# A mixture-of-experts kernel: small tables moved between partitions by ScalarE copies instead of products with selecting matrices

## The chip, the cores and the metric

The kernel runs on one core of one Trainium2 chip. The metric is the device time of one execution in microseconds (us); lower is better. Times of a kernel are given as the median of several runs, and one further execution is profiled.

## What is computed

A linear attention (eight batches, eight heads, 576 positions, 64 wide) is normalised by its root mean square and read as 4608 rows x of 512 numbers. A gating layer then decides for each row whether it is worked on at all, and which one of eight experts works on it:

```
kv  = einsum('bhsd,bhse->bhde', k, v)
o   = einsum('bhsd,bhde->bhse', q, kv)
x   = (o / sqrt(mean(o*o) + 1e-6) * g_norm)         # as rows: 4608 x 512
out = x
for rows with x @ w_skip > 0:
    e    = argmax(x @ w_gate);  gate = softmax(x @ w_gate)[e]
    out += gate * (relu(x @ w1[e]) @ w2[e])          # 512 -> 1024 -> 512, eight experts
```

## The kernel before, in words

**Attention, 0 to about 119 us.** Batches are streamed in; TensorE makes the states and the values, ScalarE squares and copies, VectorE normalises, GpSimd applies `g_norm`. The rows x are stored to `out` by SyncE's queue (lines 640 and 651) and in part by GpSimd's. The gating decisions are ranked on the way, so that at the end every chosen row has a slot of its expert.

**The experts, about 119 to 371 us.** They are done in the order of their number of rows, position r = 0 to 7. An expert's slots are cut into pieces of 128 rows, and at the end pieces of 64 or 32 rows (`PIECES`, line 279). For each piece GpSimd gathers rows of x from `out` by an indirect DMA (line 1153), TensorE transposes them (`expert_in`, line 1157), ScalarE copies the transposed tile to SBUF (lines 879 and 881), TensorE makes layer 1 and layer 2, VectorE multiplies by the gate and adds x (`result`, line 1389), and GpSimd scatters the rows back (line 1392). Expert 0 runs plainly (`layer_1`, line 1181, with a relu on ScalarE at line 1183; `layer_2`, line 1193). Experts 1 to 7 use sums of blocks, Strassen-like (`fast_1`, `fast_2`, products at line 1261), for which VectorE makes sums of weights (`w1_sums`, line 1203, `w2_sums` and `x_sums`, line 1209) and adds partial products in PSUM (line 1265); ScalarE holds copies of partial products (line 1271).

**Two tables by slot.** `srow` (128 partitions x 24 columns; column r * 3 + c is slots 128c to 128c+127 of expert r) holds the row number of each slot; `gate` holds its gate. Both come from products that place values in slots (`place`, line 760), summed by VectorE (line 818). For a piece of 128 rows that begins at a multiple of 128, its column is the list of rows as it stands. There are nine pieces for which it isn't: one of 128 rows that begins 64 slots into a column, and eight of 64 or 32 rows. A piece of 64 rows is spread over 128 partitions as two halves of each row, one of 32 rows as four quarters, so the same 64 or 32 numbers have to stand in two or four places down the partitions. `again_of(table, which)` (lines 1104 to 1124) makes these nine columns. Pieces with the same place and size make one run, of which there are five, in dictionary order: (64, 128) with one column, (64, 32) with two, (0, 64) with one, (0, 64) with two, (0, 32) with three.

In the kernel before, `again_of` writes the columns into PSUM by TensorE: for each of the four runs of 64 or 32 rows one fp32 product with a matrix `again` of 0 and 1 that selects and repeats partitions, and for the run of 128 rows two products with shifted parts of the identity. Each fp32 product shows as two rows in the profile, so one full call is 12 rows for the products and 12 for their weight loads (line 1120).

**Who calls it, and in what order.** The order of work on each engine is written by hand (`tc.manual_schedule`): every engine takes its instructions in the order in which the Python code issues them. Near the end of the attention (lines 1541 to 1563) the order is: layer 1 of expert 0 for hidden blocks 4 and 5 on the first 192 slots; `place` and `layer_2` parts; `add_pieces` completes `srow`; then `again_rows(..., range(0, 2))` for the runs that expert 0 needs soon, `slot_rows`, block 6 of layer 1, `again_rows(..., range(2, 5))`, block 7 of layer 1, nine gathers on GpSimd, more of layer 2, `gates()` (an Exp on ScalarE with a table load before it, and a chain on VectorE), and the transposes of expert 0's last two pieces. `again_rows` turns a moved column into row numbers for the cut rows, `arows` (line 1136) and `asrc` (line 1138), on VectorE.

In `experts`, for r = 0: `first_tables` runs layer 1 of expert 0 for the remaining slots with the two gate placements between; the result of piece 0; `expert_in` for expert 1's first two pieces; then `again_gates` (line 1576), which calls `again_of` for all runs and copies the nine columns from PSUM to SBUF as `agate`; the result of piece 1, which needs `agate`; on VectorE the eight `w1_sums` of expert 1; `expert_in` for expert 1's other two pieces; layer 2 of expert 0; and on VectorE the four `x_sums` of expert 1, before the results of expert 0's last two pieces.

Of the kernel before, what the change touches and what calls it, by code (L numbers as in the profile page):

```python
# [8 lines left out]
FP32 = mybir.dt.float32  # L9
# [8 lines left out]
def kernel(  # L18
# [43 lines left out]
    nc = tc.nc  # L62
# [3 lines left out]
    P = 128  # L66
# [28 lines left out]
    gat_pool = ctx.enter_context(tc.tile_pool(name="gat", bufs=1))  # L95
# [14 lines left out]
    g_ps = ps_g.tile([P, 512], FP32)  # L110
    GB = 4 * KD + 8 * G
# [89 lines left out]
    ident = keep.tile([P, P], FP32)  # L201
# [31 lines left out]
    for a in range(2):  # L233
        r = slice(a * 64, (a + 1) * 64)
        nc.vector.tensor_scalar(out=gw_b[r, :, a, :, :],
                                in0=wraw[r, :, :].rearrange("e n (u w) -> e u w n", u=2),
                                scalar1=gcol[r, 0:1], scalar2=None, op0=ALU.mult)
# [27 lines left out]
    for i, qs in enumerate((slice(0, 4 * NQ), slice(4 * NQ, FQ))):  # L265
        nc.vector.tensor_scalar(out=row_i[:, :, qs, :], in0=row_i[:, :, qs, :],
                                scalar1=upper[:, i:i + 1], scalar2=None, op0=ALU.subtract)
# [21 lines left out]
    runs = {}  # L289
    for r, off, m in sorted(res, key=lambda x: (x[0] > 0, x[1] < KEPT, x[0])):  # L290
        col = r * CK + off // P
        at_0 = r == 0 and off < 2 * P
        runs.setdefault((off % P, m, at_0), []).append((col, r, off))
    again, part_of = {}, {}
    for lo, m, _ in runs:

        if m < P and (lo, m) not in again:
            t = keep.tile([P, P], FP32, name=f"again{lo}_{m}")
            again[lo, m] = t
            for i in range(P // m):  # L300
                nc.vector.tensor_copy(out=t[:, i * m:(i + 1) * m], in_=ident[:, lo:lo + m])
        if m not in part_of:
            q_i = setup.tile([P, 1], I32, name=f"q_i{m}")
            nc.vector.tensor_single_scalar(out=q_i[:, :], in_=part_i[:, :],
                                           scalar=m.bit_length() - 1, op=ALU.arith_shift_right)
            q_f = keep.tile([P, 1], FP32, name=f"q_f{m}")
            nc.vector.tensor_single_scalar(out=q_f[:, :], in_=q_i[:, :], scalar=float(N * P // m),
                                           op=ALU.add)
            part_of[m] = q_f
    NRES = len(res)  # L310
# [7 lines left out]
    srow = keep.tile([P, NCOL], FP32)  # L318
# [3 lines left out]
        out=srow[:, :].rearrange("p (r c) -> p r c", c=CK),  # L322
        in0=beyond[:, :].unsqueeze(1).to_broadcast([P, E, CK]),
# [496 lines left out]
    def slot_rows(cols, pool, tag):  # L820

        n = cols.stop - cols.start
        rows = pool.tile([P, n], I32, tag=f"rows{tag}", name="rows")
        nc.vector.tensor_single_scalar(out=rows[:, :], in_=srow[:, cols], scalar=float(N),
                                       op=ALU.add)
        src = pool.tile([P, n], I32, tag=f"src{tag}", name="src")
        nc.vector.scalar_tensor_tensor(out=src[:, :], in0=rows[:, :], scalar=N, in1=rows[:, :],
                                       op0=ALU.is_lt, op1=ALU.mult)
        return rows, src
# [115 lines left out]
    for b in range(KNOWN // S // 4 * 4, KNOWN // S):  # L945
        nc.gpsimd.dma_start(
            out=out[b * S:(b + 1) * S, :].rearrange("(p c) d -> p c d", c=C)[:, C - 1, :],
            in_=zero)
# [18 lines left out]
    for b, n in starts.items():  # L967
        if b:
            step, counts = portions[b]
            i = 0  # L970
# [89 lines left out]
    with tc.tile_pool(name="wpool_b", bufs=1, reuse_waits="tile") as wpool_b, \  # L1060
# [40 lines left out]

        SOON = 2

        def again_of(table, which):

            ps = g_ps[:, GB:GB + NRES]
            i = 0
            for j, ((lo, m, _), cols) in enumerate(runs.items()):
                if j not in which:
                    i += len(cols)  # L1110
                    continue
                n = len(cols)
                col = cols[0][0]
                step = cols[1][0] - col if n > 1 else 1
                if m < P:
                    parts = [(slice(0, P), again[lo, m][:, :], col)]
                else:
                    parts = [(slice(0, P - lo), ident[:, lo:P], col), (slice(P - lo, P), ident[:, 0:lo], col + 1)]
                for to, lhsT, c in parts:
                    nc.tensor.matmul(out=ps[to, i:i + n], lhsT=lhsT,  # L1120
                                     rhs=table[:, c:c + (n - 1) * step + 1:step],
                                     start=True, stop=True, skip_group_check=True)
                i += n
            return ps

        def again_rows(rows, src, which):

            ps = again_of(srow, which)
            i = 0
            for j, ((_, m, _), cols) in enumerate(runs.items()):  # L1130
                n = P // m
                cs = slice(i, i + len(cols))
                i += len(cols)
                if j not in which:
                    continue
                nc.vector.tensor_scalar(out=rows[:, cs], in0=ps[:, cs], scalar1=float(n),
                                        scalar2=part_of[m][:, 0:1], op0=ALU.mult, op1=ALU.add)
                nc.vector.scalar_tensor_tensor(out=src[:, cs], in0=rows[:, cs], scalar=N * n,
                                               in1=rows[:, cs], op0=ALU.is_lt, op1=ALU.mult)
# [296 lines left out]
        def experts(pieces, widths, srcs, xt, ht, yps0, tables, group):  # L1436

            for r in range(E):
# [17 lines left out]
                if r == 0:  # L1456
                    if yps0 is not None:
                        tables = first_tables(lambda fs: layer_1(r, xt, ht, slice(KEPT, end), fs),
                                              tables)
                        result(first[0], yps0[0], xgs[0], tables, group)  # L1460
                    else:
                        layer_1(r, xt, ht, slice(0, end), range(FC))
                    enter(more[0:2])
                    if yps0 is not None:
                        tables = again_gates(tables)
                        result(first[1], yps0[1], xgs[0], tables, group)
                    do(w1_sums(r + 1))
                    enter(more[2:])
                else:
                    fast_1(r, xt, ht, end // 2, w2_sums(r), lambda: enter(more[0:1]))  # L1470
                    enter(more[1:])
# [77 lines left out]
        arows = gat_pool.tile([P, NRES], I32, tag="arows", name="arows")  # L1549
        asrc = gat_pool.tile([P, NRES], I32, tag="asrc", name="asrc")  # L1550
        again_rows(arows, asrc, range(0, SOON))
        rows, src = slot_rows(slice(0, NCOL), gat_pool, "")
        first_1(range(6, 7))
        again_rows(arows, asrc, range(SOON, len(runs)))
        first_1(range(7, FC))
        for r in range(3):
# [18 lines left out]

        def again_gates(tables):
            agate = slot_pool.tile([P, NRES], FP32, tag="agate", name="agate")
            nc.vector.tensor_copy(out=agate[:, :], in_=again_of(tables[0][1], range(len(runs))))
            return tables[0], (tables[1][0], agate)
        experts(plan, CAPS, (src, asrc), xt0, ht0, yps0, (rows, arows), "first")  # L1580

# [5 lines left out]
        with tc.If(n_rounds > 1):  # L1587
            with tc.For_i(1, n_rounds, 1):
# [8 lines left out]
                    out=left[:, :].rearrange("p (r c) -> p r c", c=CK),  # L1597
                    in0=number_f[:, :].unsqueeze(1).to_broadcast([P, E, CK]),
                    in1=caps[:, :].unsqueeze(2).to_broadcast([P, E, CK]), op=ALU.is_ge)
                nc.vector.tensor_tensor(out=srow[:, :], in0=srow[:, :], in1=left[:, :], op=ALU.mult)  # L1600
                rows, src = slot_rows(slice(0, NCOL), slot_pool, "")
# [35 lines left out]
```

## Time and profile before

| | before |
|---|---|
| median of 4 runs | 374.5 us (373.69 to 377.35) |
| the profiled execution, its own time | 373.73 us |
| its span, first to last instruction | 371.9 us |
| TensorE clock granted | 0.998 |
| busy: PE / VectorE / ScalarE / GpSimd | 360.6 / 242.8 / 145.5 / 118.8 us |
| products at line 1120 for `srow` | 12 rows, 127.9 to 130.2 us |
| products at line 1120 for `gate` | 12 rows, 149.8 to 150.8 us |
| copies that build the `again` matrices, line 301 | 10 on VectorE, 10.5 to 11.8 us |
| `agate` copy, line 1578 | 1 on VectorE, 169 ns, at 151.1 us |

How to read it: times in the trace are microseconds from the start of the span. PE is TensorE's products and PEld its weight loads, which overlap the products; DVE is VectorE, ACT ScalarE, POOL GpSimd, SP SyncE; a q behind an engine's name is its sequencer or DMA queue. A row of a timeline gives start, duration, engine, line, operation, what is written and read, and in brackets how long the engine was idle before and what ended the wait. The ends of PE's products are modelled, and some records can be missing.

### The profile page before, as it was taken

Reading aid. Unit: us, or ns where it says so; the run is one execution under the profiler, and the core shown is the slowest. Engines: PE = TensorE matmul, PEld = TensorE weight load, DVE = VectorE, ACT = ScalarE, POOL = GpSimd, SP = SyncE. Lnnn points to the kernel's source line nnn. Section 1 sums busy time; section 2 is a strip of 40 time slices with the busy share of each in tenths; the row PEclk is TensorE's granted clock in tenths of the full one; section 3 lists DMA queues with packets and bytes.
Section 4 is the critical chain, followed back from the end, with each engine's and each line's share of the span. In section 5 each row is a group of like instructions: output and inputs, shape, how many; then the busy total and the mean of one; then the engine's idle time right before and its main releaser. Section 6 shows DMA issues by size and latency. Waiting matters only on the chain.

```text
span 371.9 us, 9717 instructions
## 1 busy us (share of the span) xinstructions
PE 360.6 (97%) x3859; PEld 314.9 (85%) x3859; DVE 242.8 (65%) x630; ACT 145.5 (39%) x398; POOL 118.8 (32%) x189
## 2 busy tenths in 40 slices
PE   8999999899999998999999999999999999999994
PEld 4788998798879768589879987998988998999983
DVE  3355557767878661866847585776876876868831
ACT  2467677666767032123303511431430440441420
POOL 7036467655777071223022303303202202102003
PEclk9999999999999999999999999999999999999999
DMA  8999999999687459954617264563672672700001
GB/s 269 386 385 389 390 384 397 395 382 332 192 305 285 113 150 361 379 186 153 226 44 261 64 228 143 195 248 82 235 249 64 234 244 78 244 3 36 22 1 54
DMA packets 32808, 81.71 MB, mean 220 GB/s; under 512 B 3242, under 2 KB 3250, under 8 KB 32756
## 3 DMA queue, kind: packets, MB, share of 16 engines
q1 hardware_dynamic: 28944, 69.48, 52.8%
q0 software_dynamic: 3792, 11.53, 9.3%
q8 instruction: 32, 0.52, 0.5%
q14 instruction: 20, 0.16, 0.1%
q10 hardware_dynamic: 20, 0.02, 0.0%
HBM read 66.80 MB, written 14.48 MB: 219 GB/s over the span
## 4 chain that ended last, share of the span: by engine, by line
PE 83%; issue 6%; DMA 5%; DVE 2%; ACT 2%; POOL 1%; SPq 1%; POOLq 0%; DVEq 0%; ACTq 0%
PE bank L1261 45%; PE bank L1193 9%; PE o_ps L499 7%; PE sum_ps L380 4%; PE bank L1181 4%; PE q_ps L461 3%; PE bank L1162 2%; DMA v<-in_v_dram 2%; PE g_ps L394 2%; DMA q<-in_q_dram 2%; DMA k<-in_k_dram 1%; PE o_ps L480 1%; PE g_ps L857 1%; PE g_ps L412 1%; PE q_ps L857 1%
## 5 line engine op out<-in xcount | busy, mean ns | idle before, releaser
L1271 ACT COPY p<-bank 128x128 f32<-128x128 f32 (+6 forms) x70 | 20.8, 297 | 99.1 <-PE bank L1261 97.3
L1261 PE MATMUL bank<-xt,w 128*128 128x128 f32 (+5 forms) x336 | 55.5, 288 | 0.6 <-DVE bank L1265 0.6
L1392 POOL DMA_INDIRECT out_dram<-xg,rows x14 | 14.0, 999 | 115.4 <-DVE xg L1389 113.1
L616 POOL TENSOR_TENSOR xb<-xl,g_b 128x512 f32<-128x512 f32 x34 | 41.3, 1214 | 29.6 <-DVE rs L537 27.7
L1261 PEld LDWEIGHTS bank<-xt,w 128*128 128x128 f32 x336 | 47.0, 190 | 2.5 <-DVE bank L1265 1.8
L1265 DVE TENSOR_TENSOR bank<-bank,p 128x128 f32<-128x128 f32 (+6 forms) x70 | 23.6, 337 | 30.2 <-PE bank L1261 28.9
L499 PE MATMUL o_ps<-kvd,qT 128*128 128x146 f32 x240 | 36.0, 290 | 0.9 <-issue 0.7
L1261 PE MATMUL bank<-xs,s 128*128 128x128 f32 (+5 forms) x224 | 36.7, 288 | 0.0
L523 DVE TENSOR_REDUCE rs<-sq 128x8 f32<-128x512 f32 x36 | 24.5, 682 | 14.8 <-ACT sq L515 14.8
L499 PEld LDWEIGHTS o_ps<-kvd,qT 128*128 128x128 f32 x240 | 31.6, 189 | 1.6 <-issue 0.9
L1261 PEld LDWEIGHTS bank<-xs,s 128*128 128x128 f32 x224 | 31.1, 190 | 1.0 <-issue 0.5
L1193 PE MATMUL bank<-w,ht 128*32 128x128 f32 (+2 forms) x424 | 29.9, 313 | 0.0
L546 DVE TENSOR_TENSOR xl<-o_ps,rs 128x584 f32<-128x584 f32 x32 | 24.5, 767 | 4.3 <-DVE rs L537 0.5
L1193 PEld LDWEIGHTS bank<-w,ht 128*32 128x32 f32 (+2 forms) x424 | 18.2, 119 | 10.7 <-issue 7.6
L1261 PE MATMUL bank<-t,ht 128*128 128x256 f32 x112 | 27.0, 384 | 0.0
L1261 PE MATMUL bank<-w,ht 128*128 128x256 f32 x112 | 26.5, 380 | 0.0
L1153 POOL DMA_INDIRECT xg<-out_dram,src x14 | 14.2, 1017 | 37.3 <-DMA out_dram<-xg,rows 13.0
L515 ACT ACTIVATE sq<-o_ps 128x512 f32<-128x512 f32 x34 | 20.3, 596 | 15.0 <-PE o_ps L499 14.9
L380 PE MATMUL sum_ps<-v,k 64*64 64x64 f32 x1152 | 25.3, 222 | 0.5 <-DMA v<-in_v_dram 0.5
L1261 PE MATMUL bank<-t,hs 128*128 128x256 f32 x112 | 25.3, 379 | 0.0
L380 PEld LDWEIGHTS sum_ps<-v,k 64*64 64x64 f32 x1152 | 21.6, 134 | 3.9 <-issue 1.4
L1261 PEld LDWEIGHTS bank<-t,ht 128*128 128x128 f32 x112 | 20.8, 190 | 3.9 <-issue 1.2
(224 smaller groups left out, 677.4 us busy)
## 6 DMA issues: line engine op xcount, KB each, us to landing
w<-in_moe_w_dram SPq DMA_DIRECT2D x16, 2048.0 KB
k<-in_k_dram SPq DMA_DIRECT2D x32, 288.0 KB
v<-in_v_dram SPq DMA_DIRECT2D x32, 288.0 KB
q<-in_q_dram SPq DMA_DIRECT2D x32, 288.0 KB
out_dram<-xb SPq DMA_DIRECT2D x29, 256.0 KB
out_dram<-xb POOLq DMA_DIRECT2D x7, 256.0 KB
xg<-out_dram,src POOLq DMA_INDIRECT x16, 3.7
out_dram<-xg,rows POOLq DMA_INDIRECT x16, 2.4
```

Of the source, the lines that this page charges most:

```text
L380: nc.tensor.matmul(out=sum_ps[w * 64:(w + 1) * 64, a, u, :], lhsT=kt[r, 2 * u + w, c, :], rhs=vt[r, 2 * u + w, c, :], start=(c == 0), stop ...
L499: mm = nc.tensor.matmul(out=ps[:, w, 0:2 * PK].rearrange("p (r k) -> p r k", r=2)[:, :, cols], lhsT=qT[:, w, a, :], rhs=kvds[b % KVD][:, u ...
L515: nc.scalar.activation(out=sq[:, :, :, :], in_=heads(ps, G, G + 2 * D), func=ACT.Square)
L523: nc.vector.tensor_reduce(out=rs[:, :, :], in_=sq[:, :, :, :].rearrange("p x y (a d) -> p x (y a) d", a=2), axis=AX.X, op=ALU.add)
L546: nc.vector.tensor_tensor(out=xl[:, :, :, :].rearrange("p x y (a k) -> p x (y a) k", a=2), in0=ps[:, :, 0:2 * PK].rearrange("p x (h k) -> ...
L616: late.append((lambda eng: eng.tensor_tensor(out=xb[:, :, 4 * u * D:(4 * u + 4) * D].rearrange("p r (w x) -> p r w x", w=2), in0=xl[:, :, ...
L1153: nc.gpsimd.indirect_dma_start(out=x_of(xg, off, m), out_offset=None, in_=cut_rows(m)[:, :], in_offset=bass.IndirectOffsetOnAxis(ap=idx[:, ...
L1181: nc.tensor.matmul(out=hps[:, cols], lhsT=w_sb[r][0][:, dc, f * P:(f + 1) * P], rhs=xt[:, dc, cols], start=(dc == 0), stop=(dc == DC - 1))
L1193: nc.tensor.matmul(out=yps[q * m:(q + 1) * m, 0:n], lhsT=ht(f)[:, off:off + m], rhs=w_sb[r][1][:, f, q * n:(q + 1) * n], start=(f == 0), s ...
L1261: nc.tensor.matmul(out=out, lhsT=lhsT(i), rhs=rhs(i), start=start and i == 0, stop=i == k - 1, skip_group_check=True)
L1265: nc.vector.tensor_tensor(out=to, in0=x, in1=y, op=ALU.add)
L1271: nc.scalar.copy(out=t, in_=x)
```

## The change

`again_of` no longer uses TensorE. It takes a tile in SBUF and fills it with ScalarE copies from one group of partitions to another: two copies for the run of 128 rows (its two halves), two for each run of 64 rows, four for each run of 32. That is 14 small copies in a full call, each of 32 or 64 partitions by one to three columns. `again_rows` gets a new tile `moved` and reads it where it read PSUM; `again_gates` has the copies write `agate` itself, so VectorE's copy from PSUM goes. Of the `again` matrices only (0, 64) is still made, since `early` (line 932) uses it; the matrices for (64, 32) and (0, 32), four VectorE copies each, are gone.

```diff
-        if m < P and (lo, m) not in again:
+        if (lo, m) == (0, 64) and (lo, m) not in again:
             t = keep.tile([P, P], FP32, name=f"again{lo}_{m}")
...
-        def again_of(table, which):
-
-            ps = g_ps[:, GB:GB + NRES]
+        def again_of(to, table, which):
+
             i = 0
             for j, ((lo, m, _), cols) in enumerate(runs.items()):
-                if j not in which:
-                    i += len(cols)
-                    continue
                 n = len(cols)
-                col = cols[0][0]
-                step = cols[1][0] - col if n > 1 else 1
-                if m < P:
-                    parts = [(slice(0, P), again[lo, m][:, :], col)]
-                else:
-                    parts = [(slice(0, P - lo), ident[:, lo:P], col), (slice(P - lo, P), ident[:, 0:lo], col + 1)]
-                for to, lhsT, c in parts:
-                    nc.tensor.matmul(out=ps[to, i:i + n], lhsT=lhsT,
-                                     rhs=table[:, c:c + (n - 1) * step + 1:step],
-                                     start=True, stop=True, skip_group_check=True)
+                if j in which:
+                    col = cols[0][0]
+                    step = cols[1][0] - col if n > 1 else 1
+                    if m < P:
+                        parts = [(q * m, lo, m, col) for q in range(P // m)]
+                    else:
+                        parts = [(0, lo, P - lo, col), (P - lo, 0, lo, col + 1)]
+                    for at_p, from_p, rows, c in parts:
+                        nc.scalar.copy(out=to[at_p:at_p + rows, i:i + n],
+                                       in_=table[from_p:from_p + rows, c:c + (n - 1) * step + 1:step])
                 i += n
-            return ps
...
-            ps = again_of(srow, which)
+            moved = gat_pool.tile([P, NRES], FP32, tag=f"moved{which.start}", name="moved")
+            again_of(moved, srow, which)
...
-                nc.vector.tensor_scalar(out=rows[:, cs], in0=ps[:, cs], scalar1=float(n),
+                nc.vector.tensor_scalar(out=rows[:, cs], in0=moved[:, cs], scalar1=float(n),
...
             agate = slot_pool.tile([P, NRES], FP32, tag="agate", name="agate")
-            nc.vector.tensor_copy(out=agate[:, :], in_=again_of(tables[0][1], range(len(runs))))
+            again_of(agate, tables[0][1], range(len(runs)))
```

## The prediction, made before the result was known

> **What bounds the kernel now.** I read the page's head first, then the chain of work that ended last, then the timeline around the three places that the diff touches. The head says which engine cannot give anything away:
>
> ```profile
> span 371.9 us, 9717 instructions
> PE 360.6 (97%) x3859; PEld 314.9 (85%) x3859; DVE 242.8 (65%) x630; ACT 145.5 (39%) x398; POOL 118.8 (32%) x189
> ...
> PE 83%; issue 6%; DMA 5%; DVE 2%; ACT 2%; POOL 1%; SPq 1%; POOLq 0%; DVEq 0%; ACTq 0%
> ```
>
> TensorE is busy 97% of the span and is 83% of the chain that ended last. A product taken off it is worth its full time unless something else is then late; ScalarE, at 39%, is where the work goes. The chain, asked for 126 to 152 us, shows the removed products on it, at line 1120:
>
> ```profile
> 128.08 0.38 PE g_ps L1120 x5
> 128.46 1.41 PE bank L1181 x8
> 129.87 0.56 PE g_ps L1120 x6
> 130.43 1.41 PE bank L1181 x8
> 131.84 3.43 PE bank L1193 x8
> 135.27 0.55 PE bank L1162 x5
> 135.82 1.88 PE bank L1193 x16
> 137.69 3.47 PE bank L1181 x26
> 141.16 0.56 issue
> ...
> 149.85 1.20 PE g_ps L1120 x12
> ```
>
> The reader is to see two things. The products cost 0.38 + 0.56 + 1.20 = 2.14 us of the chain. And from 141 to 143 us TensorE stands still for reasons the profile calls "issue": 0.56, 0.18 and 0.42 us, 1.16 in all, while the table by stretches gives the DMA engines a busy share of 0.94. The timeline then shows what lies beside the products (VectorE, GpSimd, and ScalarE's wait):
>
> ```profile
> 129.91 0.33 ACT L1183 ACTIVATE ht<-bank 128x192 f32<-128x192 f32 x1 [7.11 <-PE bank L1181]
> 131.71 0.94 POOL L1153 DMA_INDIRECT xg<-out_dram,asrc  x1 [0.30 <-issue]
> 149.45 1.07 ACT L879 COPY xt<-bank 128x512 f32<-128x512 f32 x2 [0.76 <-PE bank L1162]
> 151.28 0.48 DVE L1389 SCALAR_TENSOR_TENSOR xg<-bank,agate,xg 128x256 f32<-128x256 f32 x1
> 159.54 0.75 DVE L1389 SCALAR_TENSOR_TENSOR xg<-bank,agate,xg 128x512 f32<-128x512 f32 x1 [1.13 <-PE bank L1193]
> 161.99 0.35 DVE L1265 TENSOR_TENSOR bank<-bank,p 128x172 f32<-128x172 f32 x1 [1.05 <-PE bank L1261]
> ```
>
> ScalarE is idle for 7.11 us before 129.91, and from 151.9 to 161.3. VectorE, between the `agate` result at 151.28 and the first partial sum of expert 1 at 161.99, is idle for 1.13, 0.29 (before the result at 160.58) and 1.05 us: 2.47 us of slack.
>
> **The price of one copy.** No row of before copies a few columns of SBUF to other partitions. The nearest are these, from the timeline of ScalarE:
>
> ```profile
> 6.62 0.16 ACT L224 COPY gcol<-o_ps 128x1 f32<-128x1 f32 x1 [2.91 <-PE o_ps L220]
> 6.82 0.30 ACT L226 COPY w<-gcol 128x128 f32<-128x128 f32 x1
> 7.53 0.27 ACT L229 COPY g_b<-o_ps 128x128 f32<-128x128 f32 x1 [0.42 <-PE o_ps L227]
> 60.31 0.38 ACT L406 COPY kvd<-g_ps 64x36 f32<-64x36 f32 x2
> ```
>
> One column from PSUM takes 0.16 us; 128 columns take 0.30 from SBUF and 0.27 from PSUM, so SBUF as the source adds 0.03: 0.19 us. The pair at line 406 writes two different partition halves and takes 0.38 together, so those two do not overlap; the next copy after line 224 starts 0.20 after it, 0.04 behind its end. I take 0.19 + 0.025 = 0.215 us from one copy to the next. The low end is 0.18 (four relus at line 1183 in 0.85 us, 0.29 each, so 0.18 from start to start); the high end is 0.37, the 64x256 copies of line 387, far larger than these.
>
> Here a rule weighs against the change. The Trainium skill, "VectorE: DVE Perf Modes", section "Two Vector instructions with no wait between them", says of VectorE that an instruction whose operands start in another group of 32 partitions than the one before starts only when all before it have finished; it is stated for VectorE alone, but the pair at line 406 behaves like it. "ScalarE: Activation LUTs", section "What ACT_TABLE_LOAD costs", gives 186 ns plus 0.833 ns an element with an overlap of about 93 ns back to back: by that, without the rule, 14 copies would be an estimated 1.4 us; with the rows above they are 3.0.
>
> **The change part by part.** *Set-up.* Eight copies of about 0.17 us leave VectorE at 10.5 to 11.8 us. The chain there is input DMAs until 20.9 us: nothing. If that cover were gone it would be a gain of 0.7.
>
> *Rows, first call (6 copies).* TensorE gives back 0.38. The copies wait for `srow` (126.6) on an idle ScalarE and take 6 x 0.215 = 1.3, to 127.9; VectorE's wait for TensorE ended at 128.50, so `asrc` comes about as early or 0.5 earlier. Queued behind them on ScalarE is the relu at 129.91, which they miss by 2 us. The gathers gain nothing: `asrc` was complete at 129.24, over a microsecond before the first gather started (130.36), and the gather reads `out`, whose last stores SyncE issued at 125.3 to 126.6.
>
> *Rows, second call (8 copies).* TensorE gives back 0.56. The copies stand between the relus of blocks 6 and 7: from about 129.85 they run 8 x 0.215 = 1.7, to 131.6. The relu of block 7 (131.88 before) could come at 130.9 and comes at 131.6; its reader, the last of the four pairs of 0.43 each at line 1193, needs it at about 132.9. Exp and its table load follow at 131.9, not later than the 132.2 of before. The `asrc` columns from this call are first read by the fifth gather, at 135.5, and are there by 132.6. Cost nothing; from 0.33 us a copy the cover is gone.
>
> *What is late next.* TensorE arrives at the transposes 0.94 early. The second of them needs the gather issued at 131.71; the fastest landing at line 1153 is 3.1 us after the issue, so 134.8, where TensorE would now be at 134.6. 0.25 is lost with the wake-up: 0.7 remains.
>
> *The standstill at 141 to 143 us.* The trace doesn't show what ends it. If it moves with TensorE's work, 0.7 passes; if it ends at a time set by the DMAs, up to all of it is lost. I take the first, since the weight loads that fill the DMA engines are issued after these transposes and move with them.
>
> *Gates (14 copies).* TensorE gives back 1.20; VectorE's 0.17 copy goes. The copies stand behind the two at line 879, which end at 150.5, so they run to 150.5 + 14 x 0.215 = 153.5, and the result at 151.28 starts at 153.6: VectorE is 2.3 late. Behind it wait its eight weight sums and four `x_sums`; behind the copies on ScalarE, the two at line 881, done by 154.2, before `x_sums` want them; GpSimd's scatter of piece 1 slips by 2.3 with no reader near. TensorE comes 1.2 earlier to expert 1, so VectorE is 2.3 + 1.2 - 2.47 = 1.0 behind at the first partial sum. The sum that TensorE needs first (the one with `u`, 164.33 to 164.67 before) has some 0.45 of slack before the product that reads it at about 165.1, so TensorE waits about 0.6. 1.20 - 0.6 = 0.6 remains. At 0.18 a copy the wait is 0.1; at 0.37 it is 2.8.
>
> **The sum.** 0.7 + 0.6 = 1.3 us off the profiled execution's 373.73, 372.4. That execution lies 0.8 below the median of the runs (374.5), against which the result is read: 373.2 us.
>
> **The rivals.**
> *The gain is swallowed.* The standstill ends where it ends now, so only the gates' 0.6 is left: 373.9. For it: the DMA share of 0.94, and gathers that don't move. Against it: the loads do move.
> *The copies run cheap and VectorE keeps up.* At 0.18 a copy the gates give 1.1, with 0.7 to 0.9 before: 372.5. If the whole standstill went as well, 1.16 more, it would be 371.3; only further than that is over 1%.
> *Slower: VectorE becomes the bound through a late `agate`.* Place: ScalarE's 14 copies before line 1389. TensorE's whole gain is 0.7 + 1.2 = 1.9, and the wait grows by 14 times the price per copy, so the change turns into a loss from 0.31 us a copy on. At 0.37, with 0.25 lost at block 7 as well, it is 374.5 - 1.9 + 2.8 + 0.25 = 375.7. For it: partition groups change with every copy, and no row shows that. Against it: one column in 0.16. To be 1% slower it would take about 0.57 a copy, as long as a row of 512 columns.
> *A longer standstill.* TensorE's program is shorter and other loads meet it; doubled, it costs 1.2 and ends at 374.4, within the noise.
>
> **How the numbers follow.** The forecast has 0.45 (its own range 372.3 to 374.2), the swallowed gain 0.22, cheap copies 0.10, the slower rival 0.18, the longer standstill 0.05. One per cent is 3.7 us, about what a measurement of this kernel can tell from no change. Every case but the far end of the slower one is inside it: faster by over 1% has 0.04 (cheap copies with the standstill gone and the set-up's 0.7 or more on top), slower by over 1% has 0.09, half of the slower rival, its unseen part above 0.57 a copy. The range, 371.8 to 376.9, holds the cases to 0.37 a copy and the 1 us by which the runs' median can shift (they spread by 3.7).
>
> **What would show it right or wrong.** Line 1120 gone; ScalarE copies at line 1117, 6, 8 and 14 of them, 0.19 long and 0.2 apart; the first gather still near 130.4; the second transpose at line 1162 waiting briefly; the `agate` result about 3.2 after the end of the `gate` one rather than 0.9; a wait of TensorE for VectorE of about 0.6 near 163; from expert 2 on, the same durations, shifted by 1 to 1.5. It is wrong if a copy takes over 0.3, if the standstill grows or vanishes, or if TensorE's waits for VectorE last through expert 1.

## The result, and the profile after

Over 52 runs the changed kernel took 373.77 us (371.57 to 376.35), and the kernel before 374.75 us over 78 runs beside them (373.03 to 377.62). The ratio is 0.9966, with a 95% interval of 0.9953 to 0.9979: 1.27 us less, where the prediction had taken off 1.3. The profiled execution's span is 370.0 us against 371.9.

The head of the page of the changed kernel, and the shares of its chain:

```profile
span 370.0 us, 9688 instructions
PE 358.1 (97%) x3835; PEld 312.5 (84%) x3835; DVE 242.3 (65%) x621; ACT 151.1 (41%) x426; POOL 118.7 (32%) x189
...
PE 86%; issue 6%; DMA 2%; ACT 2%; POOL 2%; DVE 1%; SPq 0%; POOLq 0%; ACTq 0%; DVEq 0%
```

TensorE is busy 2.5 us less, ScalarE 5.6 us more. The chain of the changed kernel from 125 to 153 us (start, duration, what); behind the names that the change touches, line numbers are 4 lower than before (1193 is 1189, 1181 is 1177, 1162 is 1158):

```profile
125.93 1.88 PE bank L1189 x16
127.81 2.80 PE bank L1177 x16
130.60 3.43 PE bank L1189 x8
134.04 0.74 PE bank L1158 x5
134.77 1.88 PE bank L1189 x16
136.65 4.19 PE bank L1177 x31
140.84 0.66 issue
141.50 0.29 PE bank L1177
141.79 0.10 PE g_ps L760 x3
141.88 1.04 issue
142.93 0.66 PE g_ps L760 x15
143.59 4.11 PE bank L1177 x32
147.69 0.58 PE g_ps L760 x18
148.28 1.23 PE bank L1158 x11
```

The selecting products of line 1120 are gone. But the standstill, 0.56 + 0.18 + 0.42 = 1.16 us of "issue" before, is now 0.66 + 1.04 = 1.70. ScalarE's timeline of the changed kernel shows the copies:

```profile
126.39 1.21 ACT L1117 COPY moved<-srow 64x1 f32<-64x1 f32 x6 [3.88 <-DVE srow L818]
129.34 0.33 ACT L1179 ACTIVATE ht<-bank 128x192 f32<-128x192 f32 x1 [1.74 <-PE bank L1177]
129.69 1.66 ACT L1117 COPY moved<-srow 64x1 f32<-64x1 f32 x8
...
142.98 0.85 ACT L1179 ACTIVATE ht<-bank 128x148 f32<-128x148 f32 x4 [7.72 <-PE bank L1177]
...
149.88 2.85 ACT L1117 COPY agate<-gate 64x1 f32<-64x1 f32 x14
```

6, 8 and 14 copies take 1.21, 1.66 and 2.85 us. And VectorE's timeline of the same kernel at expert 1:

```profile
148.32 0.60 DVE L818 TENSOR_TENSOR gate<-gate,g_ps 128x24 f32<-128x24 f32 x3 [3.15 <-PE g_ps L760]
...
151.52 0.48 DVE L1385 SCALAR_TENSOR_TENSOR xg<-bank,agate,xg 128x256 f32<-128x256 f32 x1 [1.81 <-ACT agate L1117]
...
160.07 0.35 DVE L1261 TENSOR_TENSOR bank<-bank,p 128x172 f32<-128x172 f32 x1 [0.50 <-PE bank L1257]
```

The gated result starts while the copies are still running (149.88 to 152.73), and at 160.07 VectorE waits for TensorE, not the other way round.

**Two kernels set against one mark.** The attention part ahead of the change ends anywhere from 125.9 to 129.8 us in the profiled executions below, which hides a change of a microsecond. So I count from one mark: the start of the first 64-row second-layer product of the second of expert 0's pieces that are begun in the attention part (`y_more`; 126.14 us before, 125.86 after). In the table, "the rest" are expert 0's remaining 148 slots (`first_tables`), the last placing product is the last of the 36 that place the gates, and expert 0's second layer is the one behind it. Microseconds after the mark:

| kernel | first layer-1 product of the rest | its relu | last placing product | expert 0's second layer | end |
|---|---|---|---|---|---|
| before | 11.48 | 17.10 | 22.61 | 25.12 | 245.80 |
| changed | 10.72 | 17.12 | 22.22 | 23.49 | 244.10 |
| rows only | 10.70 | 17.12 | 22.26 | 24.78 | 245.27 |
| gates only | 11.48 | 17.15 | 22.65 | 23.91 | 244.45 |
| needed gate last | 10.70 | 17.18 | 22.35 | 23.61 | 244.39 |
| needed gate first | 10.73 | 17.04 | 22.16 | 23.43 | 244.36 |
| no gate copies | 10.65 | 17.06 | 22.18 | 23.44 | 243.96 |
| gate copies twice, needed last | 10.71 | 17.15 | 23.91 | 25.17 | 250.20 |
| weights later | 10.67 | 17.07 | 23.80 | 25.06 | 245.57 |
| changed, gathers later | 10.74 | 12.90 | 20.11 | 21.37 | 241.71 |
| the same again | 10.64 | 11.95 | 20.01 | 21.27 | 241.47 |
| changed, last gather later | 10.72 | 12.03 | 20.10 | 21.36 | 241.40 |
| before, gathers later | 11.48 | 12.79 | 20.86 | 23.37 | 243.43 |
| gates only, gathers later | 11.49 | 12.80 | 20.86 | 22.12 | 242.16 |

The second and third columns hold the first finding. The rows' copies bring TensorE to the layer-1 product 0.76 us earlier, yet the relu of that product comes 17.04 to 17.18 us after the mark in every kernel of the upper nine, early product or late. In the kernel before it was this row:

```profile
143.24 0.85 ACT L1183 ACTIVATE ht<-bank 128x148 f32<-128x148 f32 x4 [6.74 <-remote]
```

At the last placing product 0.39 of the 0.76 is left. From there to expert 0's second layer the gates' copies save 2.51 - 1.27 = 1.24 us, whole.

My theory from here on: **about half of the rows' saving is swallowed by the standstill, the gates' passes whole, since TensorE does not wait for the late gates.** Rivals: the rows' saving passes too; the copies or the late gates cost something that a cheaper move would still bring; and for the standstill itself, the weight loads or the gathers.

### The profile page after: what moved, and what is told of

The parts are those of the page before. It is cut to its first block, busy times and chain, and to the rows that moved or that the text cites. A ratio compares the mean times of both kernels' runs of the same rounds, so it can differ in the third digit from the quotient of the medians.

```text
span 370.0 us, 9688 instructions
## 1 busy us (share of the span) xinstructions
PE 358.1 (97%) x3835; PEld 312.5 (84%) x3835; DVE 242.3 (65%) x621; ACT 151.1 (41%) x426; POOL 118.7 (32%) x189
## 4 chain that ended last, share of the span: by engine, by line
PE 86%; issue 6%; DMA 2%; ACT 2%; POOL 2%; DVE 1%; SPq 0%; POOLq 0%; ACTq 0%; DVEq 0%
PE bank L1257 45%; PE bank L1189 9%; PE o_ps L499 8%; PE sum_ps L380 5%; PE bank L1177 4%; PE q_ps L461 4%; DMA v<-in_v_dram 2%; PE g_ps L394 2%; PE bank L1158 2%; PE g_ps L412 1%; PE o_ps L480 1%; PE g_ps L857 1%; PE g_ps L403 1%; PE q_ps L857 1%; ACT sq L515 1%
```

## The experiments

**One half of the change at a time.** `again_ps` is the old function with its selecting products, for which all the `again` matrices are made as before.

```diff
 rows only:
-            again_of(agate, tables[0][1], range(len(runs)))
+            nc.vector.tensor_copy(out=agate[:, :], in_=again_ps(tables[0][1], range(len(runs))))
 gates only:
-            moved = gat_pool.tile([P, NRES], FP32, tag=f"moved{which.start}", name="moved")
-            again_of(moved, srow, which)
+            moved = again_ps(srow, which)
```

> Only the row numbers go by ScalarE copies; the gates go by TensorE products as before. Theory (TensorE time is the gain, but TensorE's standstill near 142 us ends where it ended and swallows part of what comes before it): 0.2 to 0.6 us under before, around 374.3. Rival (what is saved before the standstill passes whole): 0.9 to 1.0 under before, 373.8. Rival (copies on ScalarE cost something here): no faster than before.

Measured: 375.11 us against 375.21 before, ratio 0.9991 (0.9963 to 1.0019). After the mark it ends 0.53 us earlier than before. The interval includes both readings; the marks do not: 0.78 ahead at the first product, 0.35 at the last placing product.

> Only the gates go by ScalarE copies; the row numbers go by TensorE products as before. Theory (nothing behind the gates swallows the gain, since VectorE needs only the column of piece 1 and not all nine): 1.1 to 1.3 us under before, 373.5, as good as the whole change or nearly. Rival (the step of the prediction: TensorE waits 0.6 for VectorE): 0.6 under before, 374.1.

Measured: 372.98 us, ratio 0.9973 (0.9947 to 0.9999). After the mark 1.35 us earlier than before, 1.25 of it between the last placing product and expert 0's second layer. The gates carry the change.

**Does the order of the copies matter?** The column that VectorE reads first is the eighth to be copied in the changed kernel.

```diff
-            for j, ((lo, m, _), cols) in enumerate(runs.items()):
+            for j, ((lo, m, _), cols) in sorted(enumerate(runs.items()), key=lambda x: x[0] == last):
...
-            again_of(agate, tables[0][1], range(len(runs)))
+            again_of(agate, tables[0][1], range(len(runs)), 2)
 needed first: x[0] != last
 twice: for at_p, from_p, rows, c in parts * (1 if last is None else 2):
```

> The whole change, but in the gates the column that the result of piece 1 reads is copied last, so that VectorE waits for all 14 copies, as the prediction had it. Theory (VectorE has slack for it): the result starts 1.2 us later than in the changed kernel, near 152.7, TensorE waits 0.0 to 0.2 for VectorE in expert 1, and the time is that of the changed kernel, 1.1 to 1.3 under before. Rival (the prediction's step with all copies waited for): TensorE waits 0.6, the time is 0.7 under before.

Measured: 373.96 us, ratio 0.9976 (0.9951 to 1.0). The result starts 3.83 us after the gates are done, 2.60 in the changed kernel. ScalarE, then VectorE, in this kernel:

```profile
151.17 2.84 ACT L1119 COPY agate<-gate 64x1 f32<-64x1 f32 x14
```

```profile
154.04 0.48 DVE L1386 SCALAR_TENSOR_TENSOR xg<-bank,agate,xg 128x256 f32<-128x256 f32 x1 [3.04 <-ACT agate L1119]
...
162.01 0.33 DVE L1262 TENSOR_TENSOR bank<-bank,p 128x172 f32<-128x172 f32 x1
```

VectorE no longer waits at its first partial sum (162.01), and from expert 1's first product to its first second-layer product on sums (`t`, `hs`) TensorE needs 19.66 us in place of 19.53. So VectorE's slack is used up, and 0.13 us over. This is the place of the copies that the prediction had assumed: it priced the wait at 0.6.

> The whole change, with the gate column that VectorE reads first also copied first (run (0, 64) ahead of the others), the other 13 copies after it. In the profile of the changed kernel the gated result starts 2.60 us after the gates are done (1.70 before), because eight copies come ahead of it; here it should start about 1.2 to 1.8 us after them. Theory (TensorE does not wait for VectorE at this place): that changes no time, the ratio to the kernel before stays at that of the changed kernel, 0.9966, or 1.0 to 1.5 us faster than before. Rival (the late result still costs part of the 0.9 us): 0.5 to 0.9 us better than that, 1.8 to 2.2 us faster than before.

Measured: 373.83 us against 374.78 before, ratio 0.995 (0.9918 to 0.9981). The result starts 1.25 us after the gates, and the marks are the changed kernel's to 0.08 us up to expert 0's second layer. No time is to be had from the order.

> As the one before, but every gate copy is made twice, 28 copies, so that the result of piece 1 starts about 4 us later than in the changed kernel, near 155.5. Theory (VectorE's slack of about 1.1 us is then used up, and the rest goes to TensorE): TensorE waits about 2.9 us in expert 1, and the time is 1.5 us over before, 376.2. Rival (VectorE catches up inside expert 1 without TensorE waiting): still about 1.2 under before.

Measured: 378.16 us, ratio 1.0082 (1.005 to 1.0113): 2.95 us slower than before, twice the 1.5 that I had expected. TensorE's timeline of this kernel shows where:

```profile
144.23 5.95 PE L1178 MATMUL bank<-xt,w 128*128 128x148 f32 x32
...
164.59 1.98 PE L1258 MATMUL bank<-xs,s 128*128 128x172 f32 x8 [2.73 <-DVE xs L1206]
```

The wait of 2.73 us for VectorE's sums is the expected one (2.9). What was not expected is the rest. The first of these lines takes 5.95 us where the changed kernel takes 4.27 for the same 32 products, and after the wait expert 1 loses about 1.7 us more. Both are the granted clock. The table by stretches of this kernel (columns: PE, PEld, DVE, ACT, POOL, PEclk, DMA share, GB/s), in two cuts:

```profile
144.00:151.00 7.00, 7.00 (x67) 6.97 (x64) 1.72 (x3) 1.82 (x8) 0.00 (x0) 0.76 1.00 370
```

```profile
164.00:166.00 2.00, 1.41 (x7) 1.41 (x8) 1.98 (x5) 0.00 (x0) 0.00 (x0) 0.83 1.00 342
166.00:168.00 2.00, 2.00 (x8) 2.00 (x8) 2.00 (x6) 0.75 (x3) 1.37 (x2) 0.50 1.05 402
168.00:170.00 2.00, 2.00 (x13) 2.00 (x12) 1.05 (x3) 0.36 (x2) 1.38 (x2) 0.82 0.65 248
```

TensorE has half its clock for (0.17 + 0.50 + 0.18) x 2 / 0.5 = 3.4 us from 165.3 on, shortly after the wait of 2.73 us ends, and that costs it 1.7. The stretch at 144 us (0.24 x 7 / 0.5 = 3.4 us as well) follows the standstill and lies ahead of the edit. In all six runs of this kernel the mean clock was low, 0.987 to 0.995, against 0.994 to 1.0 in the 29 of before (the two ranges touch). So the wait has the size expected, and the clock makes it dearer. That a wait of this length brings the clock down is read from one profile and six means; no run took the wait without the clock.

**What a free move would still bring.** The tile of gates is filled with a constant, so this kernel leaves the moving of the gates out.

```diff
-            again_of(agate, tables[0][1], range(len(runs)))
+            nc.vector.memset(agate[:, :], 0.5)
```

> The changed kernel without the 14 copies of the gates: VectorE fills the tile of gates with 0.5 instead, so this kernel leaves the moving of the gates out and the cut pieces are weighted by a constant. It is the bound of what any cheaper way to move the gates could still bring. Theory (the copies lie beside TensorE's work and cost nothing): the same time as the changed kernel, 1.0 to 1.5 us faster than before, TensorE's second layer of expert 0 starting 1.3 us after the last selecting product as in the changed kernel. Rival (the 2.85 us of copies on ScalarE hold back the next expert's input or VectorE): 0.5 us or more faster than the changed kernel.

Measured: 373.31 us, ratio 0.9941 (0.9911 to 0.9972). Up to expert 0's second layer it is within 0.07 us of the changed kernel; its end is 0.14 earlier. The interval overlaps the changed kernel's 0.9953 to 0.9979; by the marks the 14 copies cost at most 0.14 us that could be got back.

**What sets the standstill?** In the changed kernel nine gathers are issued one after another from 130.1 to 141.3 us, and two loads of weights at 134.8 and 135.4 us. One kernel moves the loads, one the gathers of expert 2, both behind the last of the first 18 placing products.

```diff
 weights later:
-        load_ahead(0, landed)
...
-                place(gp, bv, t, half, t == 0, t == half)
+                placed = place(gp, bv, t, half, t == 0, t == half)
+                if t == 0:
+                    load_ahead(0, placed)
 gathers later:
-        for r in range(3):
+        for r in range(2):
             gather_all(r, plan, src, asrc)
...
+                    tc.add_manual_dep(ins.ins, behind.ins.name, WAIT, reason="layer 1 first")
...
+                if t == 0:
+                    gather_all(2, plan, src, asrc, placed)
```

> The changed kernel with the weight loads of expert 1 (w1 and w2, issued at 134.8 and 135.4 us) made to wait for the last of the first 18 placing products, some 5 to 8 us later. Nothing is left out. In every profile so far the first relu of the rest of layer 1 starts 17.10 to 17.18 us after a fixed mark (the first second-layer product of the second kept piece), whether its product was issued 11.5 or 10.7 us after that mark; TensorE's issue gaps there are 1.2 to 1.7 us. If the loads of the weights set that release: the relu moves to about 12 us after the mark, the issue gaps go, TensorE gains 1 to 1.7 us, and the time is 2 to 3 us under before unless the first weights land late (each us late at about 158 us then costs up to a us). If the gathers set it: the relu stays at 17.1 us, the gaps stay, and the time is that of the changed kernel or up to 3 us slower for late weights.

Measured: 372.31 us, ratio 0.9935 (0.9904 to 0.9966). The relu stays at 17.07 us after the mark, and TensorE still stands, 0.63 and 1.14 us. This kernel's timeline, TensorE and then ScalarE:

```profile
142.13 0.29 PE L760 MATMUL g_ps<-bv,oha_k 128*128 128x72 bf16 x4 [0.63 <-issue]
143.56 0.61 PE L760 MATMUL g_ps<-bv,oha_k 128*128 128x72 bf16 x14 [1.14 <-issue]
144.01 5.94 PE L1178 MATMUL bank<-xt,w 128*128 128x148 f32 x32
```

```profile
143.61 0.85 ACT L1180 ACTIVATE ht<-bank 128x148 f32<-128x148 f32 x4 [7.66 <-remote]
```

So it is not the weight loads, nor the DMA engines being full: their share from 137 to 144 us was 0.49 here. (The 5.94 us at 144.01 is a clock of 0.76 again, 1.7 us that the later marks of this kernel contain; it is the one reason why it ends later after the mark than the changed kernel.)

> The changed kernel with the three gathers of expert 2's pieces (issued 137.7 to 141.3 us) made to wait for the last of the first 18 placing products; the six of experts 0 and 1 stay. Nothing is left out. If the gathers set the release of the first relu: it comes when the sixth gather is through instead of the ninth, 13 to 14 us after the mark instead of 17.1, TensorE's issue gaps of 1.2 to 1.7 us shrink to under 0.5, and the time is 2 to 3 us under before. If the weight loads set it: the relu stays at 17.1 us or moves by under 0.5, the gaps stay, and the time is that of the changed kernel (the gathered pieces are not used before about 165 us).

Measured: 370.95 us, ratio 0.9882 (0.9844 to 0.9921): 3.83 us under before by the medians and 4.09 by the marks, more than the 2 to 3 that I had expected. The relu comes 12.90 us after the mark. The same chip had run three kernels with nine gathers in a row, "needed gate first", "no gate copies" and "weights later", and there it came at 17.04 to 17.07. ScalarE's first relus of the rest here:

```profile
140.76 0.48 ACT L1182 ACTIVATE ht<-bank 128x148 f32<-128x148 f32 x2 [3.50 <-PE bank L1180]
```

So with the three gathers of expert 2 out of the way the release comes 4.2 us earlier. The chain of this kernel has no "issue" left (the numbers of lines 1177, 1158 and 1189 are 3 higher here):

```profile
138.67 4.22 PE bank L1180 x32
142.89 0.58 PE g_ps L760 x18
143.47 4.11 PE bank L1180 x32
147.58 0.58 PE g_ps L760 x18
148.17 1.23 PE bank L1161 x11
```

**The test of the theory: the same edit in the kernel before, and in the half change.** If the standstill swallowed the rows' saving, it must come back whole where there is none. The edit is the one above; the chip is another one than for the edit's first run.

> The kernel before, with the three gathers of expert 2's pieces made to wait for the last of the first 18 placing products. Nothing is left out. With the changed kernel the same edit moved the first relu from 17.1 to 12.9 us after the mark and took the issue gaps away. If the standstill was what swallowed the saving on the rows, it is taken from this kernel too, and the two kernels then differ by all that the change saves on TensorE, 0.77 us for the rows and 1.25 for the gates: from the mark to the last placing product 20.9 us here against 20.1 in the changed kernel with the same edit, and on to the second layer 2.5 us against 1.26. In time this kernel should be 1.5 to 2.1 us under before, and 2.0 above the changed kernel with the same edit. If the saving on the rows was lost elsewhere (late gathers, VectorE), the two differ by 1.3 as without the edit: from the mark to the last placing product 20.4 to 20.5 us here.

> The copies for the gates alone (rows by products), with the three gathers of expert 2 made to wait as in the kernel beside it. Nothing is left out. Standstill swallowed the rows' saving: 1.25 us faster than the kernel before with the same edit, 0.7 to 0.8 slower than the changed kernel with it; mark to last placing product 20.9 us. Lost elsewhere: the same time as the changed kernel with the edit within 0.1 us by the marks, 20.1 to 20.3 us.

> The changed kernel with the three gathers of expert 2 made to wait, a second time, beside the two kernels that it is compared with. Standstill theory: 3.0 to 4.0 us faster than before (3.83 by the medians in its first run), 2.0 faster than the kernel before with the same edit. Other theory: 1.3 faster than that.

Measured, on one chip and beside the same runs of before: before with the edit 373.01 us, ratio 1.0013 (0.9986 to 1.0039); gates only with it 372.16, ratio 0.9986 (0.996 to 1.0011); changed kernel with it 370.90, ratio 0.996 (0.9937 to 0.9983). Whole change against none: 2.11 us by the medians, 1.96 by the marks (243.43 - 241.47); the theory said 2.0, the other 1.3. By the marks the gates give 1.27 of it and the rows 0.69; the medians split it the other way, 0.85 and 1.26, but the runs of one kernel spread by 2.9 to 4.0 us. To the last placing product it is 20.86, 20.86 and 20.01 us, as the theory had it. The chain of the kernel before with the edit:

```profile
139.69 4.22 PE bank L1184 x32
143.92 0.58 PE g_ps L760 x18
144.50 4.11 PE bank L1184 x32
148.61 0.58 PE g_ps L760 x18
149.19 0.90 PE bank L1165 x8
150.10 1.20 PE g_ps L1121 x12
```

No "issue" either. So in these three kernels TensorE doesn't stand still, and there the rows' saving arrives whole. For that comparison it is all one what took the standstill away.

What did not fit: the edit alone should have made the kernel before 1.5 to 2.1 us faster, and its ratio says no difference. In this set of runs the kernel before itself took 372.24 us, 2.5 less than in the earlier ones, and the same changed kernel with the edit is 3.83 us under it in one set and 1.34 in the other, at 370.95 and 370.90 us. There is no profile of before from the second chip, nor of any kernel with nine gathers in a row. With the edit the two chips agree, and without it they differ by 2.5 us, which is about what the edit takes from the kernel by the marks (2.39 in the changed kernel, 244.10 - 241.71). That fits a chip on which TensorE doesn't stand still even without the edit; it is not shown. So that the edit takes the standstill from the kernel before, too, is not shown either, and what the edit is worth on that chip is open.

**One gather alone.**

```diff
-            gather_all(r, plan, src, asrc)
+            gather_all(r, plan if r < 2 else {2: plan[2][:-1]}, src, asrc)
...
+                    gather_piece(xgs[2], plan[2][-1], src, asrc, placed)
```

> The changed kernel with only the last of the three gathers of expert 2 made to wait for the last of the first 18 placing products. Nothing is left out. Release that follows the end of the last gather issued before it (1.7 us behind it with nine gathers, 1.4 with six): with eight gathers the first relu 15.8 to 15.9 us after the mark in place of 17.1, and a part of the issue gaps gone. A release that depends on the gathers otherwise (the first of the three, say, or their number past a limit): 17.1 or 12.9 us.

Measured, on the second chip: 370.00 us against 372.24, ratio 0.9964 (0.9927 to 1.0002), five runs. The relu comes at 12.03 us, not at 15.8: my rule, a release so many microseconds behind the last gather, is wrong. ScalarE's first relus and GpSimd's last gathers in this kernel:

```profile
138.08 0.29 ACT L1182 ACTIVATE ht<-bank 128x148 f32<-128x148 f32 x1 [2.63 <-PE bank L1180]
139.09 0.29 ACT L1182 ACTIVATE ht<-bank 128x148 f32<-128x148 f32 x1 [0.71 <-PE bank L1180]
```

```profile
137.88 1.11 POOL L1150 DMA_INDIRECT xg<-out_dram,src  x1 [0.30 <-issue]
139.30 0.94 POOL L1150 DMA_INDIRECT xg<-out_dram,src  x1 [0.30 <-issue]
141.93 2.10 POOL L1150 DMA_INDIRECT xg<-out_dram,asrc  x1 [1.68 <-PE g_ps L760]
```

The relus follow the products one by one (0.71 us apart) while the seventh and eighth gathers are being issued. In the nine profiles with nine gathers in a row the first four relus come in one bunch, 5 us later by the mark. That would make it the ninth gather's own, or the number of nine. But no kernel with nine gathers in a row was profiled on this chip, so it is not shown that the relus would have been late here with the ninth in its place. What is shown is that three gathers make the difference, on the first chip; which of them, and by what means GpSimd's gathers hold back what ScalarE hears of TensorE's products, is open.

## Why the prediction was right, point by point

The total was right and two of its terms were not: 0.7 + 0.6 = 1.3 was forecast, and in the profiles 0.39 + 1.24 = 1.63 us are gained up to expert 0's second layer (1.70 to the end), against 1.27 in the times. The errors, 0.31 too much for the rows and 0.64 too little for the gates, have opposite signs; that the total came within 0.1 of the measured time is in part luck.

*The price of one copy: right.* 0.19 us long (188 to 198 ns) and 0.20 apart, for 0.19 and 0.215. 14 copies took 2.85 us. The Trainium skill's rule in "VectorE: DVE Perf Modes" (section "Two Vector instructions with no wait between them"), weighed in the prediction, is written for VectorE; these ScalarE copies, which change their partition group, behave as it says: no copy overlaps the next, while the relus of line 1179, 0.29 us long and on the same partitions, start 0.18 apart. All the copies here are small and all change their group, so the runs don't tell these two apart.

*Set-up: not shown.* It was to bring nothing. The mark lies anywhere from 125.9 to 129.8 us, which hides a gain of 0.7. (That 0.7 counts the eight copies from start to start: four take 0.43 us together, so they start 0.09 apart.)

*First and second call of the rows: right.* The first gather is issued 4.21 us after the mark, 4.22 before; the relu of block 7 (131.37) is on time.

*The transposes: right.* TensorE comes to the first of them 0.96 us earlier by the mark (8.97 to 8.01) and to the products behind them 0.77: 0.19 is lost there, for 0.25.

*The standstill: this step failed.* "If it moves with TensorE's work, 0.7 passes" was taken because the weight loads move with TensorE's work. They do, but they do not set it: with the loads 8.7 us later the relu stayed. The gathers of expert 2 do, and the gathers stay where they were by the mark (the first at 4.21 us, 4.22 before). The rival of the swallowed gain named gathers that don't move as a reason for it and had the mechanism right, though not all of the rows' gain was lost. The DMA share of 0.94, its other reason (137.6 to 143.7 us), was not the cause: with the loads late the share was 0.49 and the relu no earlier. In place of 0.7, 0.39 passed. By the prediction's own signs this part is wrong: it was to be wrong "if the standstill grows or vanishes", and it grew from 1.16 to 1.70 us.

*The gates: TensorE's side right, VectorE's wrong.* TensorE gives back 1.24, for 1.20. VectorE was to start 2.3 us late; it started 0.24 late by the profiles' own times, 0.52 by the mark (0.9 counted from the end of the gates), and TensorE shows no wait in expert 1. The step that failed is "the result at 151.28 starts at 153.6": it let VectorE wait for all 14 copies, but the result reads one column, which is the eighth to be copied. And even with all 14 ahead of it TensorE lost 0.13 us, not 0.6: the slack of VectorE was taken too small. So of the gates' gain 1.24 remained, not 0.6.

*The slower rival: its mechanism is real, its price was not reached.* With 14 copies ahead of the reader TensorE loses 0.13 us, with 28, which take 3.0 us longer, 2.73: 0.86 of each further us is paid, where the rival said all of it, and the clock came on top. But at 0.20 us a copy, with eight of them ahead of the reader, 0.50 us of VectorE's slack was still left.

## What to carry to other kernels

A product taken off the busiest engine is worth its time only as far as the next event that something else sets: mark the release times before and after it, and look for one that does not move. When a tile is filled by several small instructions, count those ahead of the column that its first reader wants, not all of them. And before a saving is called lost, compare the kernels where there is no standstill behind it: here the missing 0.4 us of the rows was then there in full. What an edit is worth on a chip shows only where the kernel is profiled there with and without it.

## What the runs showed of the hardware that I had not expected

- Nine gathers in a row on GpSimd, some 1.25 us apart, went with late news of TensorE's results at ScalarE: in all nine profiles with them the first four relus of 0.29 us came together, 17.0 to 17.2 us after the mark. TensorE issued products until 14 to 15 us after it and then stood for 0.9 to 1.8 us. With three of the nine moved, on a chip that showed the late relus three times, the first relu came at 12.90 us. On another chip the same kernel had it at 11.95, and with only the ninth moved it was at 12.03; no kernel with all nine in a row was profiled there.
- A wait of TensorE can cost more than its length: after 2.73 us of waiting its clock was halved for 3.4 us, which took another 1.7. The Trainium skill, "TensorE: Matmul & The Clock Gate", section "Part 1: The HAM clock gate", has the clock halved after an idle window of about 3.4 us. The 3.4 us of the stretch agree with it; the wait ahead of it was shorter here. In two of the nine profiled executions with the standstill (the doubled copies and the late weights) the same stretch followed that, at 144.8 us, though TensorE had stood for less than 2 us. The trace shows when that happened. The two stretches of half clock in the kernel with doubled copies begin 20.48 us apart, six times 3.41. If time is cut into such pieces of 3.41 us, counted from the first change of the clock in each profile, TensorE was idle for 0.78 of the piece ahead of the stretch at 165.3 us, and for 0.50 and 0.52 of the one ahead of 144.8 us in these two profiles. In the other seven the standstill was spread over two pieces or shorter, and filled at most 0.43 of one. So it went with how the standstill fell on these pieces. It is not the whole rule: the second profile of the changed kernel with the gathers later, which has no standstill, has its clock halved from 7.65 to 11.06 us, after a piece with TensorE idle for only 0.05 of it. The three slowest runs of the changed kernel (376.08 to 376.35 us) are those with a mean clock of 0.991 and 0.992; the others have 0.995 or more. That these, too, come from the standstill is possible and not shown: that second profile has a mean of 0.992 without one.
- One kernel's median against the kernel before came out 3.83 and 1.34 us lower in two sets of runs, all of the difference being in the kernel before (374.78 and 372.24 us). The two sets were run on two chips.
